# Another written-out order for a fused attention and gated-convolution kernel: which instruction goes when, on which engine, in which PSUM bank

## The chip, the cores and the metric

The kernel runs on one core of one Trainium2 chip. The metric is the device time of one execution in microseconds (us). The kernel before takes 236.21 us, the median of three runs (236.02 to 237.47). A profiled execution, from which every duration below is read, took 237.85 us. Engines are called as in the profile: PE is TensorE's matmul, PEld its weight load, DVE is VectorE, ACT is ScalarE, POOL is GpSimd and SP is SyncE.

## The reference

There are 8 sequences of 576 tokens. Attention has 8 heads of 64 columns, with keys and values averaged over 8 neighbouring tokens, so that each head has 72 keys. Its output, heads side by side, is the input of a feed-forward part of width 512 to 1024 to 512 with a convolution over three neighbouring tokens as its gate.

```python
k_p = k.reshape(B, H, Sp, 8, D).mean(axis=3)        # B=8, H=8, Sp=72, D=64
v_p = v.reshape(B, H, Sp, 8, D).mean(axis=3)
scores = np.matmul(q, k_p.transpose(0, 1, 3, 2)) / np.sqrt(D)
scores = scores - np.max(scores, axis=-1, keepdims=True)
attn = np.exp(scores)
attn = attn / (np.sum(attn, axis=-1, keepdims=True) + 1e-09)
x = np.matmul(attn, v_p)                            # heads side by side: (8, 576, 512)
h = np.maximum(x @ w_in, 0.0)                       # w_in 512 x 1024
conv_out = sum over 3 taps of conv_w[tap] * h shifted by tap-1 along the sequence
out = (h * sigmoid(conv_out)) @ w_out               # w_out 1024 x 512
```

Inputs and output are float32; the kernel computes in bf16 with float32 sums.

## The kernel before

**Pairs and tiles.** The sequences go in four pairs (`groups`, number g). The 1152 rows of a pair make nine tiles t of 128 rows; tile 4 holds the last 64 rows of the first sequence and the first 64 of the second.

**Attention of a tile.** Scores are TensorE matmuls (L516, or L503 in a form of 64x64 tiles). DVE takes the row maximum (L529) and subtracts it (L541; for the first pair TensorE adds the shift itself, L549). ACT takes the exponential (L567). The result is transposed, in pairs 0 and 1 by TensorE (L578) with a copy out of PSUM (L592), in pairs 2 and 3 by a transposing DMA on SP's queue (`att_send`, L587). The values follow as six matmuls (L603), DVE divides (L616, L618), and the tile is transposed into `xT`, by TensorE (L635) and a copy (L643) for sequences 0 to 3, by a transposing DMA (L627) after that.

**Keys, queries, values.** Keys of sequences 0 and 1 are pooled by TensorE with a 0/1 matrix (`prep_k`, L374 and L384) and copied to `kT` (L399). Keys of a later pair are pooled by three DVE additions and turned by TensorE (`turn_pair`), and four copies (`copy_pair`; L425) bring them to `kT`: two per sequence, both out of the same two PSUM banks, each on DVE or ACT as the order says. Queries are transposed by TensorE, in 36 instructions of 128-row form (L464) or 72 of 64x64 form (L468), and copied (L474). Values are pooled on DVE in four steps (`prep_v`).

**Feed-forward of a sequence.** `ffn_in` (L648; for sequence 0 by tiles, L669) and ACT's ReLU (L657, L679) give `hT` in eight blocks of 128 features. The convolution (L730) is written as matmuls of 64x64 tiles with diagonal weights, two feature blocks to a step, in four PSUM banks. The sigmoid is a tanh on ACT (L741) and additions and a product on DVE (L752, L755, L759). `ffn_out` (L764) takes eight matmuls of 512 columns per tile, a copy (L775, DVE or ACT) and stores on SP's queue (L787).

**Loads.** All inputs are loaded by POOL's queue (software DMA), from L251 to L287: queries q0 to q7, keys k0 and k1 (k0 in two parts, k0 and k0+; q0 too), key pairs kk1 to kk3, values v0 to v7, weights w0, w1 (the halves of w_in) and wout. POOL also builds the pooling matrix (pm), the identity (ident) and the head mask (mask) in the same stream.

**What sets the order.** The code builds a graph of some 960 operations with `add(...)`, each with the engines that it may run on, an estimated cost, what it needs, and the buffers and PSUM banks that it uses. Nothing is planned at build time: `ORDER` lists the operations as they are issued, and a number is twice the operation's index plus the choice among its engines; a negative number is a fill, a matmul on a blank tile (L367) whose result is not used. `FORMS` gives the tile form where there is a choice, `PLACES` the first PSUM bank of each token that lives in PSUM, in that order. Other buffers go round in rings (`e` 6, `eT` 3, `tg` 5, `vm` 5 and so on).

```python
for n in self.ORDER:
    o = spares.pop(0) if n < 0 else self.ops[n // 2]
    o.engine = list(o.engines)[0 if n < 0 else n % 2]
    if o.forms:
        o.mode = o.forms[next(forms)][0]
    for k in o.uses:
        if k.slots is None and k.ring == "ps":
            i = next(places)
            k.slots = list(range(i, i + k.n))
```

Each engine runs its instructions in the order in which they are issued, and waits by semaphores for what its operands need. Costs, due times and landing times given to `add` only serve the search that wrote the list; with the list given they have no effect on what is built.

Of the kernel before, what the change touches and what calls it, by code (L numbers as in the profile page):

```python
# [33 lines left out]
class Graph:  # L34
# [37 lines left out]
        70, 76, 78, 726, 72, 564, 934, 251, 728, 730, 554, 714, 936, 938, 136, 732, 894, 556, 717, 567,
        896, 138, 559, 940, 954, 578, 734, 546, 737, 580, 898, 900, 956, 548, 140, 958, 142, 902, 584, 914,
        916, 918, 582, 905, 551, 596, 586, 718, 720, 144, 146, 598, 588, 570, 942, 626, 944, 920, 600, 960,
        632, 738, 722, 572, 148, 150, 906, 740, 628, 725, 962, 946, 630, 908, 948, 575, 590, 922, 965, 966,
        925, 742, 592, 745, 594, 968, 950, 608, 970, 953, 232, 234, 973, 636, 746, 638, 642, 610, 926, 614,
        748, 750, 612, 928, 666, 616, 752, 618, 910, 913, 552, 754, 620, 930, 236, 668, 756, 560, 622, 933,
        670, 624, 634, 238, 247, 245, 243, 758, 241, 656, 1142, 760, 658, 662, 762, 765, 602, 672, 1110, 604,
        1144, 1146, 1018, 1006, 1148, 606, 1020, 1022, 1112, 640, 1114, 1008, 1010, 646, 648, 644, 1126, 660, 652, 1042,
        1150, 674, 1128, 1044, 82, 84, 1030, 1130, 677, 152, 1024, 1032, 1026, 1046, 1034, 1028, 686, 678, 1036, 1048,  # L80
        1132, 1116, 1038, 1050, 650, 154, 654, 688, 690, 680, 1040, 1012, 256, 1052, 1064, 259, 1014, 1016, 1070, 664,
        1066, 692, 264, 568, 766, 782, 156, 158, 1094, 768, 266, 1096, 1098, 1152, 1154, 771, 694, 697, 784, 787,
        284, 1074, 698, 1068, 286, 268, 682, 774, 700, 1076, 1072, 1080, 1054, 270, 685, 1078, 80, 86, 90, 702,
        704, 160, 274, 1060, 273, 277, 1056, 776, 576, 1082, 162, 1156, 279, 830, 824, 842, 832, 826, 1100, 1118,
        1134, 1102, 779, 780, 834, 828, 836, 844, 1058, 164, 838, 846, 166, 168, 170, 1062, 172, 1084, 840, 1086,
        1090, 1088, 874, 876, 878, 880, 818, 1120, 806, 820, 822, 812, 808, 810, 1122, 1092, 814, 864, 816, 280,
        848, 88, 870, 866, 1104, 850, 852, 174, 882, 282, 854, 1106, 868, 872, 260, 1136, 1138, 856, 858, 798,
        263, 860, 790, 862, 884, 1158, 800, 886, 890, 1160, 803, 292, 288, 888, 1162, 1164, 892, 1334, 1124, 1108,
        792, 788, 1166, 291, 295, 1206, 1336, 1338, 1350, 1352, 1354, 1356, 1208, 772, 1140, 1211, 1340, 1550, 804, 1168,
        1552, 1170, 982, 990, 1318, 984, 992, 987, 1554, 1320, 1322, 1302, 1304, 1306, 998, 1172, 1212, 1694, 1696, 795,  # L90
        176, 1358, 1342, 995, 1556, 1324, 1238, 1000, 1250, 1240, 1308, 1003, 1252, 1226, 1242, 1360, 1698, 1254, 1362, 1344,
        1228, 1220, 1346, 1700, 1230, 1710, 1712, 1714, 1222, 1214, 1224, 1486, 1216, 1326, 796, 1256, 1232, 1218, 1310, 1328,
        1488, 1490, 1234, 974, 178, 1716, 180, 182, 1330, 1364, 1558, 996, 988, 1348, 1258, 1718, 1492, 1236, 1260, 1502,
        1190, 1504, 1312, 976, 1192, 1314, 1195, 978, 1506, 1292, 1534, 1536, 1538, 1560, 1508, 1298, 1294, 1562, 1244, 1296,
        1198, 1518, 1520, 1522, 1316, 1332, 1196, 1246, 1404, 1004, 1524, 1702, 1182, 1406, 980, 1564, 1720, 1200, 1184, 1408,
        1540, 1542, 1248, 1203, 1722, 1186, 1262, 1268, 1264, 1272, 1300, 1278, 1434, 1274, 1704, 1436, 1428, 1438, 1440, 1430,
        1442, 1266, 1270, 1706, 1282, 1432, 1444, 1284, 1288, 1276, 1280, 1476, 1478, 1286, 1494, 1526, 1480, 1724, 1422, 1544,
        1546, 1174, 1482, 1510, 1290, 1398, 1424, 1400, 1496, 1426, 1176, 1708, 1188, 1204, 1402, 1446, 1498, 1178, 1500, 1466,
        1452, 1448, 1528, 1468, 1472, 1484, 1382, 1410, 1416, 1530, 1512, 1514, 1366, 1450, 1412, 1532, 1384, 1418, 1420, 1414,
        1368, 1390, 1456, 1516, 1548, 1387, 1470, 1370, 1372, 1474, 1742, 1180, 1388, 1744, 1746, 1462, 1458, 1374, 1636, 1726,  # L100
        1376, 1638, 1640, 1392, 1454, 1395, 1728, 1730, 1460, 1630, 1378, 1606, 1632, 1464, 1608, 1648, 1732, 1610, 1624, 1650,
        1582, 1626, 1652, 1628, 1748, 1612, 1574, 1734, 1380, 1750, 1396, 1634, 1584, 1586, 1614, 1576, 1674, 1616, 1680, 1676,
        1578, 1654, 1656, 1660, 1678, 1752, 1618, 1598, 1658, 1754, 1756, 1642, 1736, 1590, 1600, 1620, 1682, 1738, 1644, 1622,
        1592, 1594, 1664, 1603, 1646, 1666, 1670, 1684, 1690, 1686, 1668, 1672, 1688, 1662, 1692, 1740, 1832, 1802, 1834, 1808,
        1836, 1814, 1820, 1810, 1812, 1804, 1816, 1818, 1790, 1822, 1806, 1824, 1796, 1792, 1794, 1798, 1800, 1848, 1858, 1850,
        1854, 1864, 1860, 1826, 1566, 1828, 1782, 1588, 1580, 1862, 1852, 1856, 1568, 1830, 1571, 1784, 1786, 1596, 1866, 1838,
        1840, 1844, 1868, 1874, 1774, 1788, 1870, 1872, 1758, 1604, 1766, 1776, 1572, 1768, 1771, 1779, 1760, 1763, 1780, 1764,
        1772, 1842, 1876, 1846, 1878, 1894, 1902, 1896, 1899, 1880, 1882, 1900, 1886, 1904, 1907, 1888, 1891, 1884, 1908, 1892,
        1910, 1912, 1914, 1916, 1920, 1918,
    )  # L110
    FORMS = (
        0, 0, 1, 1, 0, 1, 1, 1, 0, 0, 0, 0, 0, 1, 1, 0, 1, 0, 0, 0, 0, 0, 0, 0, 0, 1, 0, 0, 0, 1, 0, 1, 0, 1, 1, 1, 1, 1, 1, 1,
        0, 0, 0, 0, 0, 0, 0, 0, 1, 0, 1, 0,
    )
    PLACES = (
        1, 2, 1, 2, 1, 2, 1, 1, 2, 3, 1, 2, 3, 1, 2, 3, 1, 0, 1, 2, 3, 0, 2, 0, 4, 5, 6, 7, 6, 7, 4, 2, 4, 0, 6, 4, 0, 1, 6, 7,
        0, 2, 0, 4, 6, 2, 4, 6, 0, 2, 4, 6, 2, 4, 6, 7, 0, 2, 6, 7, 4, 0, 2, 6, 2, 4, 6, 2, 4, 0, 2, 4, 5, 6, 0, 2, 4, 0, 2, 6,
        4, 0, 6, 2, 0, 6, 4, 2, 0, 6, 4, 3, 2, 0, 4, 3, 0, 6, 0, 4, 2, 3, 2, 6, 0, 4, 2, 0, 1, 2, 6, 4, 1, 6, 1, 2, 4, 0, 6, 1,
        0, 2, 1, 4, 6, 0, 4, 6, 2, 0, 1, 4, 6, 0, 6, 2, 4, 0, 6, 2, 4, 6, 0, 2, 4, 6, 0, 2, 4, 6, 0, 2, 4, 6, 0, 4, 2, 6, 4, 5,
        0, 2, 6, 0, 2, 6, 4, 0, 1, 2, 6, 4, 0, 6, 2, 4, 0, 2, 6, 0, 4, 2, 6, 0, 4, 2, 6, 0, 4, 6, 0, 2, 6, 4, 0, 1, 2, 4, 6, 2,  # L120
        4, 6, 0, 4, 2, 6, 4, 5, 6, 2, 0, 6, 4, 2, 0, 4, 6, 2, 4, 0, 6, 2, 4, 0, 6, 4, 7, 0, 0, 2, 4, 6, 2, 0, 4, 6, 1, 4, 2, 4,
        6, 0, 4, 2, 0, 6, 2, 4, 0, 6, 2, 4, 0, 6, 4, 2, 6, 4, 0, 6, 2, 4, 0, 6, 3, 6, 0, 4, 2, 7, 4, 0, 2, 4, 0, 6, 4, 0, 5, 2,
        6, 0, 4, 6, 2, 0, 4, 6, 1, 2, 6, 4, 0, 2, 6, 0, 4, 2, 0, 4, 2, 6, 0, 4, 2, 6, 7, 0, 2, 4, 6, 0, 1, 2, 3, 0, 1, 2, 0,
    )

# [34 lines left out]
def kernel(  # L160
# [666 lines left out]
    def soon():  # L827
        seq[0] += 0.01
        return seq[0]
# [327 lines left out]
```

## Time and profile before

| what | value |
|---|---|
| three timed runs | 236.02, 236.21, 237.47 us |
| profiled execution | 237.85 us |
| its span in the profile | 235.6 us |
| end of TensorE's last block of matmuls | 230.66 us |
| matmuls and weight loads | 3362 each in the page's count |
| DMA | 31.51 MB, of it 16.26 on POOL's queue and 14.64 on SP's |
| packets of the instruction queue q8 | 26, 0.43 MB |

The span runs from the first to the last record of the engines; the profiled execution's own time holds some 2 us more. In the page, a row of the busy table gives tenths of busy time in 40 equal slices of 5.89 us, PEclk is the clock that TensorE was granted in tenths, and DMA the busy share of the core's 16 DMA engines. In a timeline row stand the start in us, the busy time, the engine, the line and operation, output and inputs, shape and count, and in brackets the idle time of the engine just before and what ended it ("issue": nothing that the profile shows). In a row by windows stand the window's ends, its length, the busy time of each engine with the number of its instructions, the granted clock, the mean DMA share (over 1 where queues overlap) and GB/s.

The landings of the loads, in us: k0+ 5.54, k0 6.94, q0 9.36, q0+ 10.99, q1 14.07, v0 18.35, k1 21.24, q2 24.06, w0 26.84, w1 29.38, v1 31.97, kk1 38.0, q3 40.8, wout 45.9, q4 48.8, v2 51.5, v3 54.2, v4 57.0, q5 60.2, kk2 65.9, kk3 89.7, q6 94.1, v5 99, v6 101, v7 105.7, q7 109.2.

### The profile page before, as it was taken

Reading aid. Unit: us, or ns where it says so; the run is one execution under the profiler, and the core shown is the slowest. Engines: PE = TensorE matmul, PEld = TensorE weight load, DVE = VectorE, ACT = ScalarE, POOL = GpSimd, SP = SyncE. Lnnn points to the kernel's source line nnn. Section 1 sums busy time; section 2 is a strip of 40 time slices with the busy share of each in tenths; the row PEclk is TensorE's granted clock in tenths of the full one; section 3 lists DMA queues with packets and bytes.
Section 4 is the critical chain, followed back from the end, with each engine's and each line's share of the span. In section 5 each row is a group of like instructions: output and inputs, shape, how many; then the busy total and the mean of one; then the engine's idle time right before and its main releaser. Section 6 shows DMA issues by size and latency. Waiting matters only on the chain. (4 is left out here: it accounts for less than half of the span.)

```text
span 235.6 us, 7790 instructions
## 1 busy us (share of the span) xinstructions
PE 216.2 (92%) x3362; PEld 150.8 (64%) x3362; DVE 173.9 (74%) x365; ACT 146.3 (62%) x246; POOL 28.0 (12%) x45
## 2 busy tenths in 40 slices
PE   6697899969999899988998899899999999999991
PEld 2455799756678777556764477568766665875440
DVE  4489886996999999988799779769757625716510
ACT  2245668896888997749766576358434563685320
POOL 7930731110000520300000000000000000000000
PEclk9979999997999999999999999999999999999998
DMA  5999999999940299999135777656665642601596
GB/s 88 163 186 207 207 207 207 207 207 206 191 98 3 19 199 185 230 179 171 25 70 32 155 150 137 130 124 132 91 133 116 130 85 46 136 3 38 112 203 143
DMA packets 44006, 31.51 MB, mean 134 GB/s; under 512 B 23596, under 2 KB 39364, under 8 KB 43972
## 3 DMA queue, kind: packets, MB, share of 16 engines
q0 software_dynamic: 16288, 16.26, 42.9%
q1 hardware_dynamic: 27604, 14.64, 32.3%
q8 instruction: 26, 0.43, 0.8%
q10 hardware_dynamic: 80, 0.13, 0.1%
q14 instruction: 8, 0.07, 0.1%
HBM read 32.52 MB, written 9.44 MB: 178 GB/s over the span
## 5 line engine op out<-in xcount | busy, mean ns | idle before, releaser
L764 PE MATMUL psum<-w_out_sb,gT 128*128 128x512 bf16 x288 | 70.2, 382 | 0.0
L648 PE MATMUL psum<-xT,w_in_sb 128*128 128x288 bf16 x448 | 63.7, 286 | 2.3 <-ACT tg L741 2.3
L648 PEld LDWEIGHTS <-w_in_sb 128*128 128x128 bf16 x448 | 42.0, 98 | 16.5 <-issue 2.8
L657 ACT ACTIVATE hT<-psum 128x576 bf16<-128x576 f32 x56 | 35.0, 649 | 23.8 <-PE psum L648 23.6
L741 ACT ACTIVATE tg<-psum 128x576 bf16<-128x576 f32 x64 | 37.5, 652 | 12.5 <-PE psum L730 11.0
L764 PEld LDWEIGHTS <-gT 128*128 128x128 bf16 x288 | 27.0, 98 | 25.4 <-issue 0.7
L529 DVE TENSOR_REDUCE negm<-psum 128x8 f32<-128x576 f32 (+1 forms) x36 | 27.1, 752 | 5.8 <-PE psum L516 3.9
L730 PE MATMUL psum<-hT,dw 64*64 64x288 bf16 (+4 forms) x1152 | 30.3, 246 | 1.1 <-ACT eT L592 0.3
L730 PEld LDWEIGHTS <-dw 64*64 64x64 bf16 x1152 | 25.3, 107 | 8.0 <-issue 7.3
L618 DVE TENSOR_TENSOR x<-psum,r 128x512 bf16<-128x512 f32 x36 | 24.9, 692 | 1.2
L775 ACT COPY osb<-psum 128x512 f32<-128x512 f32 (+1 forms) x26 | 14.6, 581 | 16.9 <-PE psum L764 15.1
L759 DVE TENSOR_TENSOR gT<-gT,hT 128x1152 bf16<-128x1152 bf16 x32 | 24.3, 758 | 1.1
L567 ACT ACTIVATE e<-sd 128x576 bf16<-128x576 f32 x27 | 18.2, 684 | 7.9 <-DVE sd L541 4.9
L775 DVE COPY osb<-psum 128x512 f32<-128x512 f32 (+1 forms) x11 | 7.3, 667 | 19.9 <-PE psum L764 14.5
L541 DVE TENSOR_TENSOR sd<-psum,negm 128x576 f32<-128x576 f32 x27 | 20.4, 755 | 0.8
L755 DVE TENSOR_SCALAR gT<-tg 64x576 bf16<-64x576 bf16 x64 | 19.7, 309 | 1.5 <-ACT tg L741 0.2
L603 PE MATMUL psum<-vm,eT 128*128 128x130 bf16 (+5 forms) x240 | 18.4, 222 | 1.4 <-DVE negm L529 1.4
L752 DVE TENSOR_SCALAR gT<-tg 128x576 bf16<-128x576 bf16 x32 | 9.5, 305 | 11.7 <-ACT tg L741 11.6
L603 PEld LDWEIGHTS <-eT 128*128 128x128 bf16 (+1 forms) x240 | 14.5, 100 | 4.3 <-DMA eT<-e 1.5
L434 DVE TENSOR_TENSOR v<-v 128x1280 bf16<-128x1280 bf16 (+2 forms) x24 | 13.0, 542 | 0.2
L592 ACT COPY eT<-psum 128x640 bf16<-128x640 bf16 x15 | 10.3, 691 | 4.4 <-PE psum L578 4.1
L616 DVE RECIPROCAL r<-psum 128x8 f32<-128x8 f32 x36 | 7.3, 202 | 7.8 <-PE psum L603 7.6
(73 smaller groups left out, 205.9 us busy)
## 6 DMA issues: line engine op xcount, KB each, us to landing
out_dram<-osb SPq DMA_DIRECT2D x71, 128.0 KB, 2.4
v<-in_v_dram POOLq DMA_DIRECT2D x8, 512.0 KB, 18.5
qp<-in_q_dram POOLq DMA_DIRECT2D x7, 576.0 KB, 14.0
kk<-in_k_dram POOLq DMA_DIRECT2D x3, 1152.0 KB, 13.9
w_in_sb<-in_moe_w_in_dram POOLq DMA_DIRECT2D x2, 512.0 KB, 17.0
w_out_sb<-in_moe_w_out_dram POOLq DMA_DIRECT2D x1, 1024.0 KB, 20.0
kk<-in_k_dram POOLq DMA_DIRECT2D x2, 288.0 KB, 4.5
kk<-in_k_dram POOLq DMA_DIRECT2D x1, 576.0 KB, 12.8
```

Of the source, the lines that this page charges most:

```text
L529: nc.vector.tensor_reduce(out=a["m"][0:rows], in_=a["s"][0:rows, :, 0:2 * KW].rearrange("p a (h s) -> p a h s", s=Sp), axis=AX.X, op=OP.ma ...
L541: nc.vector.tensor_tensor(out=a["d"][0:rows], in0=a["s"][0:rows, :, 0:2 * KW].rearrange("p a (h s) -> p a h s", s=Sp), in1=a["m"][0:rows]. ...
L603: nc.tensor.matmul(out=a["o"][lo:hi, h // 4, (h % 4) * (D + 1):(h % 4 + x1 - x0) * (D + 1)], lhsT=a["eT"][:, j, lo:hi], rhs=buf("vm", b)[: ...
L618: nc.vector.tensor_tensor(out=a["x"][0:rows].rearrange("p (a h d) -> p a h d", a=2, d=D), in0=ov[:, :, :, 0:D], in1=r[0:rows].unsqueeze(3) ...
L648: nc.tensor.matmul(out=banks(ps)[:, j, 0:SC], lhsT=w_in_block(dc, fb), rhs=buf("xT", g)[:, dc, i * S + j * SC:i * S + (j + 1) * SC], start ...
L657: nc.scalar.activation(out=buf("hT", b)[:, fb, :].rearrange("p (a s) -> p a s", a=2), in_=banks(ps)[:, :, 0:SC], func=ACT.Relu, scale=0.5,)
L730: nc.tensor.matmul(out=banks(pss[r ^ c])[c * D:(c + 1) * D, j, lo:hi], lhsT=dw[r * D:(r + 1) * D, tap * n_fb + fb, :], rhs=hT[r * D:(r + 1 ...
L741: nc.scalar.activation(out=tg.rearrange("p (a s) -> p a s", a=2), in_=banks(ps)[:, :, 0:SC], func=ACT.Tanh, scale=0.5,)
L755: nc.vector.tensor_scalar(out=gate[r * D:(r + 1) * D, fb], in0=tg[(1 - r) * D:(2 - r) * D], scalar1=1.0, scalar2=None, op0=OP.add)
L759: nc.vector.tensor_tensor(out=gate[:, both], in0=gate[:, both], in1=buf("hT", b)[:, both], op=OP.mult)
L764: nc.tensor.matmul(out=bank(ps)[0:rows, :], lhsT=buf("gT", g)[:, fb, t * P:t * P + rows], rhs=w_out_sb[:, fb, :], start=(fb == 0), stop=(f ...
L775: copy(out=osb[0:rows, columns], in_=bank(ps)[0:rows, columns])
```

## The change

`ORDER`, `FORMS` and `PLACES` are replaced as a whole. The other edits are to costs that the list was once searched with. The diff, with the lists cut to their beginnings:

```diff
     ORDER = (
-        18, 4, 2, 0, 26, 8, 10, 16, 12, 30, -1, -1, -1, -1, -1, -1, -1, -1, -1, -1,
-        -1, -1, -1, -1, -1, -1, -1, 92, 98, 102, 24, 14, 34, 97, 101, 95, 58, 20, 32, 104,
...
+        10, 14, 6, 2, 24, 16, 12, 20, 8, 28, 22, -1, -1, 36, 18, 26, 108, 4, 40, 104,
+        111, 34, -1, 107, 30, -1, 32, 92, 58, 56, 94, 97, 98, 64, -1, 48, 100, -1, -1, 103,
...
     FORMS = (
-        0, 0, 1, 1, 0, 1, 1, 1, 0, 0, 0, 0, 0, 1, 1, 0, 1, 0, 0, 0, 0, 0, 0, 0, 0, 1, 0, 0, 0, 1, 0, 1, 0, 1, 1, 1, 1, 1, 1, 1,
-        0, 0, 0, 0, 0, 0, 0, 0, 1, 0, 1, 0,
+        0, 0, 1, 1, 0, 0, 1, 1, 0, 0, 0, 1, 1, 0, 1, 1, 1, 0, 1, 0, 0, 0, 0, 0, 0, 1, 0, 0, 0, 1, 0, 1, 0, 1, 1, 1, 1, 0, 1, 1,
+        1, 0, 0, 0, 0, 0, 0, 0, 1, 0, 1, 1,
     PLACES = (
-        1, 2, 1, 2, 1, 2, 1, 1, 2, 3, 1, 2, 3, 1, 2, 3, 1, 0, 1, 2, 3, 0, 2, 0, 4, 5, 6, 7, 6, 7, 4, 2, 4, 0, 6, 4, 0, 1, 6, 7,
...
+        0, 2, 3, 1, 2, 3, 4, 1, 2, 1, 4, 5, 2, 4, 1, 6, 1, 1, 2, 0, 4, 5, 6, 7, 6, 7, 2, 3, 5, 5, 2, 6, 4, 0, 2, 6, 0, 2, 4, 5,
...
-    LATE = 2.0
+    LATE = 1.8
-    c1 = add({"DVE": 0.6}, soon(), clear_pool_matrix)
+    c1 = add({"DVE": 1.5}, soon(), clear_pool_matrix)
-    cwp = add({"PE": 0.1}, soon(), lambda: turn_conv_weights(cwtok), after=[idf, cwl], uses=[cwtok])
-    zv = add({"DVE": 0.55}, soon(), lambda: clear(*[v0[TB:P, 4, :] for v0 in buffers["v"]]))
+    cwp = add({"PE": 0.1}, soon(), lambda: turn_conv_weights(cwtok), after=[idf, cwl], uses=[cwtok], count=2)
+    zv = add({"DVE": 0.84}, soon(), lambda: clear(*[v0[TB:P, 4, :] for v0 in buffers["v"]]))
-    zk = add({"DVE": 0.8}, soon(), lambda: clear(*buffers["kT"][1:]))
+    zk = add({"DVE": 1.25}, soon(), lambda: clear(*buffers["kT"][1:]))
-    dw0 = add({"DVE": 0.2}, soon(), lambda: build_conv_matrices(0, cwtok), after=[cwp], uses=[cwtok])
+    dw0 = add({"DVE": 0.3}, soon(), lambda: build_conv_matrices(0, cwtok), after=[cwp], uses=[cwtok])
-    picked = add({"DVE": 0.5}, START + Graph.DW - 1, build_pick, after=[c0])
+    picked = add({"DVE": 0.95}, START + Graph.DW - 1, build_pick, after=[c0])
-            o = add({"SP": 1.29}, key, lambda: att_send(g, t), after=[o, ze], uses=[e, eT], land=(1.7, 0, 1))
+            o = add({"SP": 1.29}, key, lambda: att_send(g, t), after=[o, ze], uses=[e, eT], land=(2.1, 0, 1))
-            o = add({"SP": 1.29}, key, lambda: att_out(g, t), after=[o], uses=[x, xtok[g]], land=(1.7, 0, 1))
+            o = add({"SP": 1.29}, key, lambda: att_out(g, t), after=[o], uses=[x, xtok[g]], land=(2.1, 0, 1))
-                       after=relu[fbs[0]] + relu[fbs[1]] + dwo, uses=cbs + tgs + [htok[b], gtok[g]], mode=QUARTER, count=64 + 12 * i)
+                       after=relu[fbs[0]] + relu[fbs[1]] + dwo, uses=cbs + tgs + [htok[b], gtok[g]], mode=QUARTER, count=64 + 16 * i)
```

What the two lists make of it, counted in the built programs: fills go from 25 to 18, with 2 ahead of the first other work on TensorE where there were 17. POOL's stream was k0+, k0, ident, pm, q0, q0+, q1, v0, k1, mask, q2, w0, w1, v1, kk1, q3, wout, q4, v2, v3, v4, q5, kk2, kk3, q6, v5, v6, v7, q7; it becomes q0, k0, ident, pm, mask, k0+, q0+, v0, q1, k1, q2, w0, v1, w1, kk1, q3, q4, wout, v2, v3, kk2, v4, q7, v5, q5, kk3, q6, v6, v7. The query transposes have 324 instructions of 64x64 form before and 360 after, the scores 144 and 176; TensorE's stream has 6739 and then 6810 instructions. One query copy and one `eT` copy go from ACT to DVE. The twelve copies of `copy_pair` were eleven on ACT and one on DVE, the one on DVE out of the banks that ACT read at the same time; now all are on ACT. Where the two kernels share code, the changed one has it one line higher up.

## The prediction

> **What bounds the kernel now.** I read the page first, then the busy times by stage, TensorE's waits, and the timeline around its longest gaps.
>
> ```profile
> span 235.6 us, 7790 instructions
> PE 216.2 (92%) x3362; PEld 150.8 (64%) x3362; DVE 173.9 (74%) x365; ACT 146.3 (62%) x246; POOL 28.0 (12%) x45
> PEclk9979999997999999999999999999999999999998
> DMA  5999999999940299999135777656665642601596
> ```
>
> TensorE bounds it; no other engine is over 74%. Two slices have a lowered clock, and the DMA engines are full for the first 11 of 40 slices. The busy times by stage (time, PE, PEld, DVE, ACT, POOL, clock, DMA share, GB/s) show where TensorE idles:
>
> ```profile
> 22.00:43.00 21.00, 19.91 (x453) 18.16 (x450) 17.07 (x37) 13.72 (x20) 7.39 (x10) 1.00 1.24 207
> 43.00:56.00 13.00, 10.63 (x238) 7.74 (x234) 10.82 (x24) 10.62 (x19) 1.77 (x2) 0.87 1.24 207
> 56.00:100.00 44.00, 42.90 (x686) 32.05 (x688) 42.23 (x79) 37.59 (x64) 6.46 (x9) 1.00 0.82 137
> 100.00:131.00 31.00, 27.46 (x591) 19.34 (x581) 27.61 (x60) 21.60 (x36) 0.00 (x0) 1.00 0.69 100
> 131.00:217.00 86.00, 85.01 (x1125) 58.15 (x1123) 57.46 (x117) 48.88 (x84) 0.00 (x0) 1.00 0.52 104
> ```
>
> Busy matmuls overlap, so I count in blocks of the timeline that follow each other without a gap: 4 matmuls of L764 take 0.86 us start to start, 4 of L648 0.49, a convolution block of L730 0.78, scores 0.25, values 0.36, turns 0.22 to 0.28. Without the fills of L367 these add up to 194.65 us of work. TensorE's last block ends at 230.66, so it loses 36.0 us. I call time minus work done the lag: 17.1 at the first L669 block (27.91), 17.4 at 43, 23.1 at 56, 31.9 at 131, 36.0 at the end. So half is lost before the pipeline fills, 5.6 in the convolutions of sequence 0, and 13.0 after 56 us. The largest gaps, in the timelines of 44 to 53, 103 to 108 and 124 to 131 us:
>
> ```profile
> 45.83 0.44 PE L730 MATMUL psum<-hT,dw 64*64 64x288 bf16 x11 [0.22 <-issue]
> 49.88 0.28 PE L635 MATMUL psum<-ident,x 128*128 128x128 bf16 x2
> 51.76 0.29 PE L635 MATMUL psum<-ident,x 128*128 128x128 bf16 x2 [1.60 <-issue]
> ...
> 105.06 0.46 DVE L425 CAST kT<-psum 64x288 bf16<-64x288 f32 x1
> 105.61 0.69 ACT L425 CAST kT<-psum 64x288 bf16<-64x288 f32 x2 [1.77 <-DVE kT L425]
> 106.20 0.65 ACT L741 ACTIVATE tg<-psum 128x576 bf16<-128x576 f32 x1
> 106.90 1.39 PE L648 MATMUL psum<-xT,w_in_sb 128*128 128x288 bf16 x10 [1.76 <-ACT tg L741]
> ...
> 130.19 0.38 PEld L603 LDWEIGHTS <-eT 128*64 128x64 bf16 x12 [1.53 <-DMA eT<-e]
> ```
>
> At 105 ACT may not read a PSUM bank until DVE has, its next tanh is late, and TensorE waits for that tanh's bank. At 130 it waits for a transposing DMA: the tile's view has "DMA to landing us min/median/max: 2.6/2.9/10.1", 10.1 for one issued at 83.89 behind the loads of 79 to 83. At 45.3 and 49.9 it waits for nothing but "issue". These two places are instructions 1474 and 1730 of its stream, 256 apart, and the instruction queue's 16 KB packets ran at 43.52 and 49.43. All 26 such packets fit one rule: crossing 256k-62 asks for the next block. Asked at 40.77, usable at 45.83 (5.1 us); asked at 45.83, usable at 51.76 (5.9). With the loads gone it took 3.5 (122.55 to 126.1).
>
> Half clock, from the busy times by window (time, PE, clock, DMA share, GB/s):
>
> ```profile
> 11.50:14.90 3.40, 2.96 (x25) 0.50 1.17 182
> 15.00:52.40 37.40, 32.23 (x779) 1.00 1.23 206
> 52.50:55.80 3.30, 3.30 (x36) 0.50 1.24 207
> ```
>
> The second falls on work that nothing else delays, so it costs 3.4/2 = 1.7 us.
>
> **The change part by part.** The edited costs only guided the search for the order; no instruction takes other time by them. What changes is the order, some engines, tile shapes, banks and fills. I read it from the built programs.
>
> Work. Seven fills fewer are not work by my count. One more query transpose in 64x64 form saves 0.63-0.34 = 0.3; two more scores in that form (0.24 for 0.25) and the two copies moved from ACT to DVE (1.12 and 0.69 there, 0.75 and 0.48 here) cost nothing, being hidden behind TensorE. Work is 194.3: **-0.3**.
>
> The first 24 us of work. POOL now issues q0 and k0 first, and the second half of k0 only after the 0.8 us mask, at about 5.9 instead of 1.3. Loads go through in order, 2.6 to 3.1 us for 1.18 MB, so what follows k0+ lands about 0.9 later than in the same place before. Scores start near 11.5 (10.34). But v0 is now ahead of q1 and should land at 14.7 to 16.2 (18.35); its four DVE steps (0.82, 0.49, 0.32, 0.66) and one 0.75 reduction between them let the first values start at 18 to 19.5 (21.43). DVE divides (0.93 each) and key load k1 (21.24 before, 21.2 to 22.1 now) hold the next part. Block 3 is crossed 3.0 us of work after block 2, so at least 5.4 us later in time, about 27. First L669 block: 28 to 29, with 2.0 us more work behind it, lag 15.2 to 16.5. Then w1, issued behind v1 now, lands at 31.7 to 33.2 (29.38) and is wanted after 3.5 us of work, near 32: lag 15.4 to 16.9, I take 16.4 as the load bound is the firmer row. Before: 17.4. **-1.0** (-2.0 to -0.4).
>
> Convolutions of sequence 0. Blocks 5 to 7 held 7.0 us of work and took 11.0. Now they hold 2.3 and 3.2 us, and the loads (wout, v2, v3) still run, so twice the 5.1 to 5.9 of the two rows: 2 x 5.4 - 5.5 = 5.3 lost. ACT's tanh and copies, which alone make this stage 3.3 late, fit mostly under it; 0.4 stays. A window that idles half goes to half clock as at 49 to 52: 1.5 (0 to 1.7). Sum 7.2 against 5.6: **+1.6**. Bounds: if fetches hide, 3.3, so -2.3; if both take 5.9 and the clock 1.7, 8.4, so +2.8.
>
> The rest. For every TensorE block I added the rows of the chain that releases it (through ACT's and DVE's queues, within 5 us of work) and compared it with the work between. In the order of before the largest excess of each cluster sums to 11.6, the 2.35 at 105 us among it, plus 1.4 for the slow transpose at 130: 13.0, which is what the lag shows. In the new order: 0.25, 0.94, 0.52, 1.39, 0.42, 0.30, 0.54, 0.83, 0.75, 0.2, 0.6, 0.52, 0.32, 0.31, some small, 8.2 in all. No pair of key copies is split between ACT and DVE after sequence 0. From scores to values over a DMA transpose lie at least 9.1 us of work (5.4 at the 130 us gap; the chain is 0.41+0.75+0.76+0.68+2.9 and queues). Late next is ACT: tanh waits of 0.5 to 1.4. Block 13 holds only 2.9 us, fetched in 3.5: 0.3 more. 8.5 against 13.0: **-4.5**. Bounds: 6 (every small excess absorbed) and 12.5 (new late landings as large as those seen).
>
> Tail: the last copies (0.42, 0.37, one bank) and stores are the same: 0.
>
> Sum -0.3-1.0+1.6-4.5 = -4.2. The profiled execution took 237.85 for its 235.6 span, above the median 236.21 of the timed runs; 237.85 becomes 233.65, the median **232.0**.
>
> **Two pages against it.** The TensorE page of the Trainium skill (TensorE: Matmul & The Clock Gate, Part 1) says the clock starts at half and rises only after a busy window of about 3.4 us. Fills at 0.43 apart until 4.7 us and 0.22 after agree. The new order has 2 fills at the start for 17, which by that rule leaves the start at half clock; that is the third rival below. The Trainium skill's Runtime: NRT & Kernel Launch, Instruction fetch mechanics, calls crossing a 16 KiB boundary mostly hidden. The gaps at 1474 and 1730 disagree; by the page the sum would be that of the first rival.
>
> **The rivals.** Measured against 236.2, 1% (2.4 us) is about what can be told from no change.
> - Fetches hide (stage 3.3 instead of 7.2, -3.9): 228.1. For it: block 8 and all after 110 us show no issue gap. Against: both gaps under load. 0.12.
> - The order does not do what it is for: stalls move. Blocks 3, 6, 7 and 13 each a fetch of 5.9, 2.5 more than counted, and one more window of half clock, 1.7: 236.2. For it: four short blocks where before had two under load. 0.25.
> - Slower, by the clock alone: without the early fills TensorE stays at half from the start to the first L669 tiles and again through the convolutions. Four windows there, 0.7 of them on the path, cost 4 x 1.2 = 4.8; two more later 3.4: 240.2. It decides from the fourth window that nothing else hides (6.6 us). Against it: seven fills together before tile 2's shift, 3.0 us at half clock, fill one window. 0.13.
>
> **How the numbers follow.** The forecast has 0.5, its own range 230 to 234. Faster by over 1% (below 233.85): 0.5x0.92+0.12+0.25x0.08 = 0.60. Slower (above 238.6): 0.25x0.08+0.13x0.92 = 0.14. Same: 0.26. The range 228.5 to 237.0 leaves out most of the slow rival and half of the first, under 2 in 10.
>
> **What would show it.** TensorE's last block ends near 226.4. First L669 row at 28 to 29. Two "issue" gaps of 2 to 3 us between 42 and 54, none of DVE kT before ACT kT, no wait of TensorE for eT. Wrong if key loads land later than 12, if PEclk is low in over three slices, or if waits for tg after 56 us exceed 9 us.

## The result, and the profile after

The changed kernel takes 238.48 us, the median of 20 runs (236.53 to 240.32); the kernel before, in 20 runs beside it, 236.3 (235.26 to 238.63). The ratio is 1.0058, 95% interval 1.0031 to 1.0086: a little slower (by the two medians 0.9%), where 232.0 and a gain were forecast. Medians here and below are over all executions, while the ratios leave out those more than 1.5% above the fastest of their kernel: one of the 20 here, and 5 of 12, 3 of 9 and 4 of 12 in the runs r2, r10 and r15 below. The profiled execution took 236.53, the fastest of the 20, so part of what the change usually costs is not in its trace. It was profiled a second time for that reason (237.77).

The page of the changed kernel, its first profiled execution:

```profile
span 234.3 us, 7838 instructions
PE 212.5 (91%) x3374; PEld 150.2 (64%) x3397; DVE 174.5 (74%) x367; ACT 144.0 (61%) x244; POOL 27.6 (12%) x45
PEclk9999999997999999999999999999999999999999
DMA  5999999999978199991269335767694511902486
```

One low slice of the clock for two, TensorE still the bound, and the loads run on into two more slices (7 and 8 where there were 4 and 0). The busy times by stage, with the columns and windows as before:

```profile
22.00:43.00 21.00, 19.08 (x460) 16.82 (x455) 16.33 (x29) 13.45 (x20) 6.02 (x8) 1.00 1.23 207
43.00:56.00 13.00, 9.00 (x272) 7.35 (x273) 9.95 (x24) 10.14 (x17) 3.12 (x4) 0.91 1.24 208
56.00:100.00 44.00, 42.90 (x644) 32.09 (x647) 42.50 (x79) 37.48 (x69) 6.40 (x9) 0.99 0.97 159
100.00:131.00 31.00, 28.93 (x632) 21.23 (x633) 28.81 (x62) 20.60 (x35) 0.00 (x0) 1.00 0.64 106
131.00:217.00 86.00, 84.95 (x1123) 57.71 (x1133) 57.60 (x122) 50.49 (x88) 0.00 (x0) 1.00 0.50 97
```

From 43 to 56 TensorE is busy for 9.00 us where it was for 10.63, with more instructions (272 for 238); from 100 to 131 for 28.93 where it was for 27.46. So the convolutions of sequence 0 lose and the stretch at 105 gains. TensorE's timeline of the losing stage:

```profile
43.05 1.02 PE L467 MATMUL psum<-ident,qp 64*64 64x64 bf16 x72
43.88 0.57 PE L729 MATMUL psum<-hT,dw 64*64 64x288 bf16 x3
45.52 1.92 PE L729 MATMUL psum<-hT,dw 64*64 64x288 bf16 x62 [1.07 <-issue]
...
49.38 0.53 PE L463 MATMUL psum<-ident,qp 128*64 128x128 bf16 x12
51.66 0.36 PE L463 MATMUL psum<-ident,qp 128*64 128x128 bf16 x6 [1.76 <-issue]
```

Both gaps end by "issue", at instructions 1475 and 1730 of TensorE's stream, where they were at 1474 and 1730 before. From crossing to crossing it takes 40.66 to 45.52 and 45.52 to 51.66: 11.0 us for 5.5 us of work, where the kernel before had 7.0 us of work in the same 11.0.

The lag (time minus work done, by the same block times as in the prediction) in two profiled executions of each kernel. The second of the kernel before took 236.44:

| lag, us | before | before, again | after | after, again |
|---|---|---|---|---|
| after 20 us of work (feed-forward tiles of sequence 0) | 17.8 | 17.9 | 17.2 | 18.1 |
| after 35 us (its convolutions done) | 23.1 | 21.5 | 24.8 | 24.6 |
| after 75 us | 26.4 | 25.1 | 28.1 | 28.1 |
| after 100 us | 31.9 | 30.3 | 32.0 | 32.3 |
| after 145 us | 34.5 | 33.1 | 33.7 | 34.0 |
| after 150 us | 34.5 | 33.1 | 33.7 | 34.9 |
| after 195 us, the end | 36.0 | 35.1 | 35.5 | 36.2 |
| span | 235.6 | 234.2 | 234.3 | 235.5 |

The spans of the first profiles differ by -1.3, those of the second by +1.3. Neither pair alone is the effect; the timed runs decide.

### The profile page after: what moved, and what is told of

It is laid out like the page before. It is cut to its first block, busy times and chain, and to the rows that moved or that the text cites. A ratio compares the mean times of both kernels' runs of the same rounds, so it can differ in the third digit from the quotient of the medians.

```text
span 234.3 us, 7838 instructions
## 1 busy us (share of the span) xinstructions
PE 212.5 (91%) x3374; PEld 150.2 (64%) x3397; DVE 174.5 (74%) x367; ACT 144.0 (61%) x244; POOL 27.6 (12%) x45
## 4 chain that ended last, share of the span: by engine, by line
PE 68%; DMA 13%; DVE 8%; issue 4%; ACT 2%; POOL 2%; DVEq 0%; ACTq 0%; POOLq 0%
PE psum L763 25%; PE psum L647 20%; PE psum L729 9%; DMA w_in_sb<-in_moe_w_in_dram 7%; PE psum L602 4%; DMA v<-in_v_dram 4%; PE psum L668 2%; PE psum L515 2%; DMA xT<-x 2%; ACT tg L740 2%; PE psum L634 1%; DVE x L617 1%; PE psum L577 1%; DVE negm L528 1%; PE psum L467 1%
## 5 line engine op out<-in xcount | busy, mean ns | idle before, releaser
L763 PE MATMUL psum<-w_out_sb,gT 128*128 128x512 bf16 x268 | 67.4, 380 | 1.6 <-issue 0.6
L647 PE MATMUL psum<-xT,w_in_sb 128*128 128x288 bf16 x448 | 62.6, 286 | 1.2 <-DMA xT<-x 0.5
L647 PEld LDWEIGHTS <-w_in_sb 128*128 128x128 bf16 x448 | 42.4, 98 | 14.6 <-issue 1.7
L729 PE MATMUL psum<-hT,dw 64*64 64x288 bf16 (+4 forms) x1152 | 30.7, 246 | 2.9 <-issue 1.6
L751 DVE TENSOR_SCALAR gT<-tg 128x576 bf16<-128x576 bf16 x32 | 9.4, 303 | 14.6 <-ACT tg L740 14.6
L433 DVE TENSOR_TENSOR v<-v 128x1280 bf16<-128x1280 bf16 (+2 forms) x24 | 12.9, 539 | 0.3 <-DMA v<-in_v_dram 0.2
L473 ACT COPY qT<-psum 128x1152 bf16<-128x1152 bf16 (+2 forms) x10 | 9.1, 928 | 6.4 <-PE psum L463 4.8
## 6 DMA issues: line engine op xcount, KB each, us to landing
w_in_sb<-in_moe_w_in_dram POOLq DMA_DIRECT2D x2, 512.0 KB, 17.2
kk<-in_k_dram POOLq DMA_DIRECT2D x1, 576.0 KB, 12.9
```

Source lines behind the costliest of these rows:

```text
L647: nc.tensor.matmul(out=banks(ps)[:, j, 0:SC], lhsT=w_in_block(dc, fb), rhs=buf("xT", g)[:, dc, i * S + j * SC:i * S + (j + 1) * SC], start ...
L729: nc.tensor.matmul(out=banks(pss[r ^ c])[c * D:(c + 1) * D, j, lo:hi], lhsT=dw[r * D:(r + 1) * D, tap * n_fb + fb, :], rhs=hT[r * D:(r + 1 ...
L763: nc.tensor.matmul(out=bank(ps)[0:rows, :], lhsT=buf("gT", g)[:, fb, t * P:t * P + rows], rhs=w_out_sb[:, fb, :], start=(fb == 0), stop=(f ...
```

## The experiments

Ratios are to executions of the kernel before that ran beside the changed ones, with 95% intervals: r1 to r4 have one such set, r5 to r8, r9 to r12 and r13 to r17 one each (medians 236.53, 236.50, 236.61 and 236.28). "Long" and "short" transposes are the 128-row and 64x64 forms.

| run | what | median us | ratio |
|---|---|---|---|
| r1 | changed kernel again | 237.96 | 1.0072 (1.0038 to 1.0107) |
| r2 | changed, three long transposes | 235.44 | 0.9935 (0.9901 to 0.9968) |
| r3 | before, three short transposes | 237.82 | 1.0055 (1.0024 to 1.0085) |
| r4 | before, key pair on ACT | 234.50 | 0.9922 (0.9892 to 0.9953) |
| r5, r12 | changed, early fills | 236.71, 236.95 | 1.0002 (0.9970 to 1.0035), 1.0008 (0.9977 to 1.0039) |
| r6 | r2 with the early fills | 236.85 | 1.0005 (0.9971 to 1.0039) |
| r7 | changed, gap in the loads | 246.72, one run | |
| r8 | r4 with one long transpose | 234.17 | 0.9901 (0.9864 to 0.9937) |
| r9 | changed, sixth output buffer | 237.02 | 1.0015 (0.9986 to 1.0044) |
| r10 | r2, sixth output buffer | 235.32 | 0.9907 (0.9869 to 0.9946) |
| r11 | r8, sixth output buffer | 234.14 | 0.9882 (0.9848 to 0.9916) |
| r13 | changed, one store earlier | 237.41 | 1.0035 (0.9997 to 1.0072) |
| r15 | r2, one store earlier | 235.20 | 0.9903 (0.9864 to 0.9942) |
| r16 | before again | 236.44, one run | |
| r17 | changed, w1 ahead of v1 | 237.72 | 1.0067 (1.0033 to 1.0101) |

### The fetch of instructions: r1, r2, r3, r7

r1 is the changed kernel unaltered.

> The changed kernel, unaltered, for another profiled execution. Its median of 20 runs is 238.48 us but the execution profiled so far took 236.53, its fastest: 2 us of its usual time are in no trace yet. Theory A (instruction fetch under load): the stretch from 40.7 us to the first block after the convolutions of sequence 0 took 11.0 us for 5.5 us of work; here it takes 12 to 13.5 and everything else agrees within 0.7 us. Theory B (later waits): that stretch takes 11.0 again and the 2 us lie in TensorE's waits after 56 us, by tanh results or transposing DMAs that land later. Theory C (loads): the front is longer, the first feed-forward block starts 1.5 to 2 us later than 28.6 with keys and values landing later. Time 238 to 239 by all three.

Measured: 237.96 (median), the profiled execution 237.77. The stretch took 41.54 to 52.95, 11.4 us, so theory A's 12 to 13.5 is missed; with no half clock behind it, the stage as a whole lost less than in the first profile (6.5 for 7.6). The extra time lies in the start (below), 0.9 of lag, and in one wait near 178 us, 0.9: C and B hold a part each.

r2 changes three entries of the forms, r3 three others in the kernel before:

```diff
 r2, FORMS of the changed kernel
-        0, 0, 1, 1, 0, 0, 1, 1, 0, 0, 0, 1, 1, 0, 1, 1, 1, 0, 1, 0, 0, 0,
+        0, 0, 1, 1, 0, 0, 1, 1, 0, 0, 0, 1, 1, 0, 1, 0, 0, 0, 0, 0, 0, 0,
 r3, FORMS of the kernel before
-        0, 0, 1, 1, 0, 1, 1, 1, 0, 0, 0, 0, 0, 1, 1, 0, 1, 0, 0, 0,
+        0, 0, 1, 1, 0, 1, 1, 1, 0, 0, 0, 0, 0, 1, 1, 1, 1, 1, 1, 0,
```

> The changed kernel with three query transposes of the convolution stage of sequence 0 (both halves of sequence 3, the second of sequence 4) back in 128-row form: 108 instructions fewer in TensorE's stream there and 3 x 0.3 = 0.9 us more work. Theory A: 108 of the 512 instructions of the two blocks fetched under load are gone, so 0.21 x 11.0 = 2.3 us less in the stretch, 0.9 of work back, time 1 to 2 us below the changed kernel (about 237). Theory B (nothing is bound by fetching): 0.9 more work, time the same to 0.9 above (238.5 to 239.4).

> The kernel before with three query transposes of the same stage (second half of sequence 3, both of sequence 4) in 64x64 form: 108 instructions more there and 0.9 us less work. Theory A: the two blocks fetched under load hold less work, the stage takes 1.0 to 2.3 us more, time 236.3 to 238. Theory B: 0.9 us less work, 235.4 to 236.3.

Measured: r2 is 2.5 us below r1 beside it (235.44 against 237.96) with 0.9 us more work, somewhat more than the 1 to 2 expected; r3 is 1.3 above the kernel before (237.82 against 236.53) with 0.9 us less. The rival had both signs the other way round. In r2's profile the lag at the end of the stage is 20.9 (24.6 to 24.8), and no "issue" gap is left in its rows of matmuls; TensorE's stage from 43 to 56 in r2:

```profile
43.00:56.00 13.00, 11.43 (x242) 8.51 (x240) 12.41 (x28) 11.68 (x21) 3.12 (x4) 1.00 1.24 207
```

11.43 us busy with 242 matmuls, for 9.00 with 272. The two blocks still take 11.5 us from the first crossing (instruction 1218) to the last (1730), but more work stands in them: the gaps in the rows of matmuls sum to 1.8 us, for 3.5 in the changed kernel.

r7 moves three loads in POOL's stream, so that none runs from 45 to 49 us:

```diff
 POOL, order of issue
-        q3, q4, wout, v2, v3, kk2, v4
+        q3, q4, kk2, wout, v2, v3, v4
```

> The changed kernel with the loads of wout, v2 and v3 issued behind that of the key pair kk2, which waits for its buffer until about 49 us: no load runs between about 45 and 49. Its time will be longer (wout is wanted at 56 and lands at about 58 to 60). What counts is the time from one crossing of an instruction block to the next in the convolutions of sequence 0. Theory A (the fetch is slowed by the loads): the second of the two, 6.1 us in both profiles of the changed kernel, falls to 3.5 to 4.5, the first (asked at 41, loads running) stays near 5. Rival (the fetch takes that long by itself, or the waits there are ACT's and DVE's): both stay, 5 and 6.

Measured: from crossing to crossing 41.78 to 45.67 and 45.67 to 49.86. The busy times of these two stretches, first in r7, then in the changed kernel:

```profile
41.80:45.60 3.80, 3.23 (x131) 2.34 (x132) 3.55 (x7) 2.69 (x5) 0.00 (x0) 1.00 0.69 120
45.70:49.80 4.10, 3.84 (x126) 3.19 (x127) 3.83 (x11) 3.85 (x7) 0.00 (x0) 1.00 0.02 6
```

```profile
40.70:45.50 4.80, 3.21 (x131) 2.33 (x132) 4.46 (x10) 3.45 (x5) 0.00 (x0) 1.00 1.23 208
45.50:51.60 6.10, 4.12 (x128) 3.33 (x127) 4.89 (x12) 4.79 (x10) 1.87 (x3) 1.00 1.24 207
```

The same instructions take 6.1 us at 207 GB/s and 4.1 to 4.2 at 6. The first block takes 4.9 and 3.9; it was expected to stay near 5, but here too the loads ran for a part of it only (120 GB/s). The packets of the instruction queue show where the time goes: in the changed kernel they ran 2.6 and 3.7 us after the two crossings, in r7 1.6 and 1.1, and each took 0.95 to 0.98 itself. r7's timeline of the stage:

```profile
44.16 1.02 PE L467 MATMUL psum<-ident,qp 64*64 64x64 bf16 x72
44.99 2.60 PE L729 MATMUL psum<-hT,dw 64*64 64x288 bf16 x65
47.85 0.94 PE L729 MATMUL psum<-hT,dw 64*64 64x288 bf16 x31 [0.26 <-ACT tg L740]
48.72 0.45 PE L577 MATMUL psum<-ident,e 128*128 128x128 bf16 x5
49.10 0.47 PE L411 MATMUL psum<-pick,kk 128*64 128x64 bf16 x18
49.53 0.69 PE L463 MATMUL psum<-ident,qp 128*64 128x128 bf16 x18
```

Where the first gap was, 65 matmuls follow without one; where the second was, all 18 transposes run in 0.69; a single wait, of 0.26 for a tanh, is left. Theory A holds: loads at full rate slow the fetch, and that costs 11.0 - 3.9 - 4.2 = 2.9 us in the changed kernel. The two blocks still take 8.1 us for their 5.5 of work in r7, so 2.6 of the 5.5 lost there do not hang on the loads. (r7 itself is 10 us slower; wout, wanted at 56, lands at 64.9.) That the packets follow instruction 256k-62 holds at these crossings but not everywhere: after 110 us of the changed kernel six of the 26 ran 0.4 to 2.4 us ahead of it. The Trainium skill (Runtime: NRT & Kernel Launch, Instruction fetch mechanics) says that the cost of crossing a 16 KiB boundary is mostly hidden: that is what r7 shows without loads (no "issue" gap in the rows of matmuls), and not what the changed kernel shows under them (1.07 and 1.76).

### The bank shared by ACT and DVE: r4, r8

r4 is the kernel before with a single number of its order changed, which puts the one key-pair copy of DVE on ACT.

```diff
-        704, 160, 274, 1060, 273, 277, 1056,
+        704, 160, 275, 1060, 273, 277, 1056,
```

> The kernel before with the one key-pair copy that DVE had (sequence 6) on ACT as the other three of that pair, so that no two engines read those banks; nothing else. By the prediction the wait at 105 us (1.77 of ACT for DVE, 1.92 of TensorE for the tanh behind it) goes, less about 0.7 for the added copy on ACT: 0.8 to 1.9 us faster. Rival: ACT is late by the added copy anyway and TensorE waits as long: within 0.4 us.

Measured: 234.50 for 236.53, 2.0 us faster (by the interval 1.1 to 2.6), just above the 0.8 to 1.9 expected. Its profiled execution took 238.14, with half clock at 52 and at 151 us, so its trace is used only here, around 105 us. ACT in the second profile of the kernel before, then in r4:

```profile
99.25 1.19 ACT L741 ACTIVATE tg<-psum 128x576 bf16<-128x576 f32 x2 [1.12 <-PE psum L730]
...
104.11 0.69 ACT L425 CAST kT<-psum 64x288 bf16<-64x288 f32 x2 [1.77 <-DVE kT L425]
104.70 0.65 ACT L741 ACTIVATE tg<-psum 128x576 bf16<-128x576 f32 x1
```

```profile
100.47 1.19 ACT L741 ACTIVATE tg<-psum 128x576 bf16<-128x576 f32 x2 [1.12 <-PE psum L730]
...
103.21 0.39 ACT L425 CAST kT<-psum 64x288 bf16<-64x288 f32 x1 [1.07 <-PE psum L412]
103.62 0.65 ACT L741 ACTIVATE tg<-psum 128x576 bf16<-128x576 f32 x1
104.17 0.68 ACT L425 CAST kT<-psum 64x288 bf16<-64x288 f32 x2
104.74 0.66 ACT L741 ACTIVATE tg<-psum 128x576 bf16<-128x576 f32 x1
```

The wait of 1.77 for DVE is gone. The tanh behind the two copies starts 4.27 us after the pair of tanh in the first row, where it started 5.45 after, so 1.2 earlier, and TensorE's stall behind it falls from 1.92 to 0.63. That is 1.3 of the 2.0; the rest is within the interval. So this part of the change was read rightly, and it can be had alone.

r8 adds one long transpose (first half of sequence 3, a 1 turned to 0 in `FORMS`).

> The kernel before with the copies of the last key pair all on ACT (234.50 by itself, its middle four runs 234.07 to 234.90) and the one query transpose of the convolution stage that had 64x64 form there (first half of sequence 3) in 128-row form: 36 instructions fewer under load, 0.3 us more work. Fetch theory: 36/256 of 5.5 us less 0.3, 0.5 faster than that: 234.0. Rival: 0.3 slower, 234.8.

Measured: 234.17, between the 234.0 of the fetch theory and the 234.8 of the rival; the 0.3 of difference to r4 is less than the intervals tell apart.

### The start: r5, r6, r12, r17

In r1 the first 14.6 us run slower than in the first profile of the same kernel. TensorE in the first profile, then in r1:

```profile
10.24 0.75 PE L373 MATMUL psum<-pm,kk 128*64 128x144 bf16 x18 [0.96 <-DMA kk<-in_k_dram]
11.77 0.66 PE L515 MATMUL psum<-kT,qT 128*128 128x144 bf16 x8
12.36 0.75 PE L463 MATMUL psum<-ident,qp 128*64 128x128 bf16 x20
```

```profile
9.81 1.29 PE L373 MATMUL psum<-pm,kk 128*64 128x144 bf16 x18 [0.94 <-DMA kk<-in_k_dram]
12.28 1.17 PE L515 MATMUL psum<-kT,qT 128*128 128x144 bf16 x8
13.38 1.28 PE L463 MATMUL psum<-ident,qp 128*64 128x128 bf16 x20
```

The same instructions take 1.7 to 1.8 times as long, although the granted clock is recorded as 1.00 in both: the half cadence of a start does not show in that column. The traces hold no clock record before a grant of the full clock at 9.34 us in the one and at 14.55 in the other, and that is where the half cadence ended in these two executions of one and the same kernel. The Trainium skill (TensorE: Matmul & The Clock Gate, Part 1) says that the window which decides on the clock runs freely, so that the number of slow first matmuls varies from run to run; the two profiles agree (9.34 and 14.55). r5 and r12 are the changed kernel with twelve fills more:

```diff
-        10, 14, 6, 2, 24, 16, 12, 20, 8, 28, 22, -1, -1, 36, 18, 26, 108, 4, 40, 104,
+        8, 10, 14, 6, 2, 24, 16, 12, 20, 28, -1, -1, -1, -1, -1, -1, -1, -1, 22, -1,
+        -1, 36, 18, 26, 108, 4, 40, 104,
...
-        92, 58, 56, 94, 97, 98, 64,
+        92, 58, 56, 94, 97, -1, -1, -1, -1, 98, 64,
```

> The changed kernel with 8 fills ahead of TensorE's first work and 4 between the two key poolings of sequence 0, the blank tile cleared first on DVE; 24 more instructions in the stream, no other work. In the second profile of the changed kernel TensorE's matmuls ran at half their usual cadence until 14.6 us (18 key poolings in 0.96 for 0.53 us, 10 transposes in 0.43 for 0.24), in the first until 9; in the kernel before until 4.7. Theory (late warm-up): the start is at full cadence by 6 us in every execution, the third scores start at 14.8 or before instead of 16.3, 0.8 to 1.6 us less than the changed kernel's median (236.5 to 237.5). Rival (the start is bound by loads): no more than 0.4 us less.

> The changed kernel with the early fills once more, because its profile fell on an execution of 539 us that tells nothing; its median was 236.71 against 238.0 to 238.5 without. Theory (warm start): matmuls at full cadence by 9 us and the first feed-forward block 0.8 to 1.6 earlier than 30.5 to 31, stage of the convolutions 6.5 to 7.5 lost as in the changed kernel. Rival (the 24 instructions only move the block boundaries): the front ends as late as without fills, and the convolutions of sequence 0 lose 1 to 2 less.

Measured: 236.71 and 236.95, 1.0 to 1.8 below the two medians of the changed kernel. In r12's profile those 18 poolings take 0.75 and the 20 transposes 0.75, and the third scores are at 15.70 (16.33 in r1). But the first feed-forward row is at 29.99 (29.42 and 30.71 without fills) and the lag there 17.6 (17.2 and 18.1). So a warm start is worth 0.5 us on the path by r12 against r1, and at most 0.9 by the two executions of the changed kernel; where the rest comes from, the traces do not settle.

> Both edits that may help the changed kernel: the early fills, and three query transposes of the convolution stage of sequence 0 in 128-row form (108 instructions fewer, 0.9 us more work), which alone gave 235.44. If the two are independent, another 0.8 to 1.6 less: 233.8 to 234.6. If the early part is then waited for by loads (queries of sequence 2, weights, which land at 25 to 33 us whatever the start), 235 to 235.6.

Measured: 236.85, 1.4 above r2. The fills that help the changed kernel hurt r2: their 24 instructions move every boundary of a block, and in r6's profile the second crossing is once more a gap (50.52 to 52.36, 1.84; 0.06 in r2), the lag after the stage 22.4 for 20.9. The profiled execution took 238.36, above the median, so this is one part of the 1.4 and perhaps not all. Edits to a stream of instructions are not independent of each other while boundaries under load matter.

r17 moves one load, w1 ahead of v1.

> The changed kernel with the second half of w_in (w1) loaded ahead of v1 instead of behind it, as in the kernel before. Theory (w1's landing at 33.3 sets the end of the front): w1 lands at 30.4 to 31, TensorE's wait of 0.4 for it goes, and the lag at the end of the feed-forward tiles of sequence 0 falls by 0.4 to 1.0; time 0.4 to 1.0 less than 238.0 to 238.5. Rival (v1, then landing at 33.3, takes its place through DVE's pooling of it, 2.3 us, and the values of tile (0,4) near 36): no gain, or up to 0.5 slower.

Measured: 237.72, no gain that can be told. w1 lands at 31.0 and v1 at 33.9, and the lag is 17.9: the rival, its first half.

### The store behind transposes: r9, r10, r11, r13, r15

In several profiles of the changed order, but not its first, TensorE loses 0.8 to 2.35 us near 178. ACT in r2's profile, then SP's queue:

```profile
173.09 1.19 ACT L740 ACTIVATE tg<-psum 128x576 bf16<-128x576 f32 x2 [2.00 <-PE psum L502]
176.62 1.07 ACT L774 COPY osb<-psum 128x512 f32<-128x512 f32 x2 [2.34 <-DMA out_dram<-osb]
```

```profile
164.99 3.94 SPq L626 DMA_TRANSPOSE xT<-x  x2
169.02 1.18 SPq L786 DMA_DIRECT2D out_dram<-osb  x2
170.26 1.29 SPq L626 DMA_TRANSPOSE xT<-x  x1
171.59 1.23 SPq L786 DMA_DIRECT2D out_dram<-osb  x2
```

ACT's copy for tile (2,2) goes to the buffer of tile (1,1). (The two copies of the row at 176.62 are those of (2,2) and (1,5); the first one waits.) In the changed kernel's first profile that tile is copied at 149.2 to 149.8 and its store issued at 174.3, 24.5 later (11.5 in the kernel before), since the store stands in SP's queue behind transposes that wait for their own data. It landed at 177.99 and the next copy started at 178.12: on time by 0.13 us. In r2 the store landed at 176.52 and ACT had been ready 2.3 earlier. r9 gives the ring a sixth buffer:

```diff
-    rings = {..., "osb": 5,
+    rings = {..., "osb": 6,
-    ident_f = const.tile([P, P], FP32, name="ident_f")
-    cw_raw = const.tile([3 * n_fb, P], FP32, name="cw_raw")
+    ident_f = buffers["osb"][0][:, 0:P]
+    cw_raw = buffers["osb"][1][0:3 * n_fb, 0:P]
```

> The changed kernel with six output buffers in the ring osb for five (the identity in float32 and the raw convolution weights share two of them, to make room); the order is untouched. In profiles of the changed kernel's order ACT's copy of tile (1,5) waits near 178 us for a store of tile (1,1) that stands in SP's queue behind transposing DMAs, and TensorE waits for the bank behind that copy: 0 in the first profile, 0.8 in the second, 2.35 and 2.1 with edits elsewhere. Theory (store behind transposes): the wait goes in every execution, 0.8 to 1.6 us below the changed kernel's 238.0 to 238.5. Rival (the next wait, tanh or bank, stands right behind): less than 0.4.

Measured: 237.02, 0.9 to 1.5 below the two medians of the changed kernel, as the theory had it, though the intervals of the ratios overlap; its executions lie between 236.13 and 237.67 (the changed kernel's between 236.53 and 240.32). There is no wait near 178 in its profile, but there was none in the first profile of the changed kernel either.

> The changed kernel with the three 128-row query transposes (235.44 by itself) and the sixth output buffer: if the two are independent, 233.8 to 234.8; if not, 235.2 to 235.6. In the profile no wait of over 0.5 us near 178.

Measured: 235.32, as r2, so the two do not add. The wait was not gone: in its profile, one of its slower executions (237.92), the copy one place on, (1,5), waits 1.80 us for the same store.

> The kernel before with the key pair on ACT, the one 128-row transpose (234.17 together) and the sixth output buffer. There DVE's copy of tile (1,0) waited at 145 us for the store of (1,1), issued 2.4 us earlier behind stores and transposes, and TensorE lost 1.6 behind it. Theory: 233.0 to 233.6, no wait of over 0.8 near 146. Rival: nothing gained, 234.2.

Measured: 234.14, as r8. DVE's wait at 145 is gone and another took its place: TensorE waits 1.4 us, until 150.41, for a transposing DMA into `xT`. The rival.

r13 and r15 leave the buffers and move the store itself:

```diff
 SP, order of issue
+        store (1,1) directly behind store (1,0)
...
-        store (1,1) behind the transposes of (3,0), (3,1) and (3,2)
```

> The changed kernel with one operation of SP's queue moved: the store of output tile (1,1), copied at 149.8 us but issued at 174.3 behind four transposing DMAs, now stands right behind the store of (1,0), near 159. Theory (that store holds back ACT's copy near 178, and TensorE behind it): 0.8 to 1.5 us below the changed kernel's 238.0 to 238.5, and its slowest executions (239 to 240) gone. Rival (its 1.2 us of issue in SP's queue delays the transposes behind it, or the next store takes its place): within 0.4.

> The same move beside the three 128-row query transposes (235.44 by itself, with 2.35 us lost near 178 in its profiled execution): 234.0 to 234.8 if the two add; 235.2 to 235.6 if not.

Measured: r13 237.41, r15 235.20, which is what was expected if the two do not add. Neither profile has a wait of over 0.5 near 178; r15's lag grows by 0.1 from 140 to 150 us of work, for 2.5 in r2. So the traces show that the late store made the wait. By the times it is not shown to matter: its share is 0.6 to 1.1 in the changed kernel, which the intervals do not separate from none, 0.2 by the medians of r2 and r15, and 240.06 still occurs in r13.

### The kernel before once more: r16

> The kernel before, unaltered, for a second profiled execution: the first took 237.85, above the median. Theory (part of the forecast gain was the first execution's bad luck): TensorE's wait for the transposed exponentials of tile (2,4) near 129 us is 0.56, as in the kernels derived from it, not 1.58; the stretch of half clock at 52.5 to 55.9 is there again, since it was in two of the derived kernels that leave that stage alone. The wait at 105 us is 1.92 again. Time 235.5 to 237.

Measured: 236.44. ACT's wait at 105 is there again (1.77, and 1.92 on TensorE). The transpose at 129 is as late as in the first profile:

```profile
128.59 0.38 PEld L603 LDWEIGHTS <-eT 128*64 128x64 bf16 x12 [1.43 <-DMA eT<-e]
```

so that was no bad luck of one execution, and my theory fell there. The half clock at 52 is not there although both gaps of the fetch are, so such a gap does not always bring it; without it the lag after the stage is 21.5 for 23.1.

## Why the prediction was wrong, step by step

- **Work, -0.3.** The built programs have it (194.3 for 194.65); no run isolates it.
- **The first 24 us of work, forecast -1.0.** Wrong: -0.6 and +0.2 in the two pairs of profiles. The steps to it held: scores from 11.8, v0 at 16.1, w1 at 33.3, at the edge of its range. What failed is the end, the first row of the feed-forward (L669, here L668) at 28 to 29: it came at 29.4 and 30.7, 1.7 behind the crossing of block 3 as in the kernel before (26.2 and 27.9). Block 3, forecast at about 27, was crossed at 27.8 and 29.1. Its fetch was not longer than counted (5.0 us in both, for 5.4); block 2 was reached late, at 22.8 and 24.0, where the forecast implies 21.6. I took the lower bound of each chain and only one wait behind them, and counted the missing fills in a rival, not in the sum.
- **The convolutions of sequence 0, forecast 7.2 lost, +1.6.** Right in place and mechanism: 7.6 and 6.5 lost; 5.3 and 3.6 before. In the two blocks 5.3 of loss by fetching was forecast and 5.5 is lost (11.0 for 5.5 of work), but by r7 only 2.9 of it goes with the loads; that the sum came out is in part luck. r2, r3 and r7 show the cause, and with three transposes back in the long form (r2) the new order is 1.1 us faster than the old by the medians. Like for like the stage is +2.3 and +2.9. The half clock that I added (1.5) came in the first profile and not in the second, and in the kernel before likewise: it belongs to the execution, not to the order.
- **The rest, forecast 8.5 lost against 13.0, -4.5.** This is the step that failed. 10.7 and 11.6 were lost, against 12.9 and 13.6: -2.2 and -2.0. The named waits went, as forecast: no ACT kT waits for DVE kT after 30 us, and r4 shows it worth 2.0; no tile waits for eT (longest landing 5.5 and 6.3 us, 10.1 and 10.0 before). Mis-sized were the new ones. Block 13, taken as fetched in 3.5 us for 2.9 of work as if no load ran, took 4.2 and 4.9, with DMA at 150 and 165 GB/s in that stretch: 0.7 to 1.4 more. The stores behind transposes were in no term: 0 to 2.35 near 178. What is left, 1.5 us in the first profile and about 0.8 in the second, is spread over small waits that no run isolates (TensorE's waits for a tanh sum to 0.7 in both). In the order of before the method gave 13.0 and the lag 13.0, but the slow transpose had been put in by hand from the trace: a sum of excesses that fits the order it was read from is not yet a forecast for another.
- **The base.** The sum was made against the profiled execution of 237.85, whose half clock (1.7 in the prediction, 1.6 between the two lags) was counted as lying in every execution. The second profile of the kernel before does not have it.
- **The tail, forecast 0.** From the end of TensorE's last block to the end of the span it took 4.9 and 4.5 us before, 4.5 and 5.0 after: executions of one kernel differ as much as the kernels.
- **The signs.** None of the signs of being wrong came: the last part of the keys of sequence 0 landed at 10.2, the clock was low in one slice of each profile, and TensorE waited 0.7 us for tanh results after 56 us. They watched neither block 2 nor block 13 nor the stores. Of what was to show the forecast, the two "issue" gaps came, of 1.07 and 1.76 us for 2 to 3, and TensorE's last block ended at 229.8 and 230.5 for 226.4.
- **The rivals.** "Stalls move" gave 236.2, the slow one 240.2; 238.48 lies between, 2.3 from the one and 1.7 from the other, and neither was right. "Stalls move" took 5.9 us for each of four fetches; the two profiles show 5.0 and 5.0 (to block 3), 4.9 and 5.3, 6.1 and 6.1 (the convolutions), 4.2 and 4.9 (block 13). The slow one had a mechanism that exists, the start at half cadence, but it wanted half clock up to the first L669 tiles, and it ended at 9.3 and 14.6; its price was 4.8 us there and the fills recover 1.0 to 1.8. "Fetches hide" is what r7 shows without loads, and only there.

Of the 6.5 us between 232.0 and 238.48, 2.3 to 2.5 are the rest, 0.4 to 1.2 the front, 0.7 to 1.3 the convolutions; the remainder, 1.5 to 3.1, is in no block of these traces, and its cause stays open. The profiled executions of the changed kernel were 2.0 and 0.7 faster than its median, those of the kernel before 1.6 and 0.1 slower than its own. Best of all by its median is r11, 234.14 us (ratio 0.9882), but r8 does as much with two numbers changed in the kernel before.

## What to carry to other kernels

While loads run at full rate, count instructions per microsecond of TensorE's work: a form with half the instructions and 0.3 us more work was the faster one here, and anything that shifts the stream by a few instructions moves the gaps. Look, in every queue, for an instruction that is ready long before its turn: a store that waited 24.5 us behind transposes (25.7 in r2) held a buffer, which held ACT, which held TensorE. And profile a kernel twice before a sum is made against one execution.

## What the hardware did that I had not expected

- One block of 256 instructions of TensorE took 4.9 to 6.1 us to come with loads at 207 GB/s, and at most 3.9 to 4.2 with fewer or none; block 13 took 4.2 and 4.9 at 150 and 165. What grew under load was the time until the block's packet ran (3.7 us for 1.1), not the packet (0.95 and 0.98).
- TensorE ran at half cadence until 14.6 us while the column of the granted clock says 1.00; the trace has no clock record before that time.
- A store of 128 KB lands 2.3 us after its issue at best, and up to 4.5 in r2 with transposing DMAs around it (164.30 to 168.76 us; the one that ACT waited for took 4.3, 172.22 to 176.52).
